# A fused attention, gated layer and 8-expert layer: new order tables, expert operands inside the order, last first-layer column in expert PSUM banks

## The chip, the cores and the metric

The kernel runs on one core of a Trainium2 chip. The metric is the device time of one execution in microseconds (us), the median over several runs. PE is TensorE (matmuls), DVE is VectorE, ACT is ScalarE, POOL is GpSimd, SP issues the DMAs.

## What is computed

Three stages, one behind the other, on 1152 tokens of width 512:

```python
def _moe_ref(x, w_gate, w_val, w_out):
    gate = 1.0 / (1.0 + np.exp(-(x @ w_gate)))
    val = x @ w_val
    return (gate * val @ w_out).astype(np.float32)

def _moe2_ref(x, w_gate, w1, w2):          # N=1152, D=512, E=8, F=1024
    logits = x @ w_gate
    P = np.exp(logits - logits.max())
    for _ in range(8):
        P /= P.sum(1, keepdims=True) + 1e-09
        P /= P.sum(0, keepdims=True) + 1e-09
        P *= N / E
    out = np.zeros((N, D), dtype=np.float32)
    for e in range(E):
        h = np.maximum(x @ w1[e], 0.0)
        out += P[:, e:e + 1] * (h @ w2[e])
    return out.astype(np.float32)

def reference(q, k, v, moe, moe2):
    x = _attn_ref(q, k, v)                 # softmax attention, queries pooled by 2
    x = _moe_ref(x, *moe)                  # the first layer
    return _moe2_ref(x, *moe2)             # the expert stage
```

## The kernel before

**Number format.** Every fp32 operand of a matmul is held as a pair: a high part (an ACT copy that rounds to the matmul's format) and a low part (source minus high part, a DVE or POOL subtraction). Such a pair is called a split here. A product then takes three matmuls: high x high, high x low, low x high (`three`, L835 to L837; in the second product L1281, L1285, L1286).

**Stages.** Attention comes first and is not touched. The first layer follows: gate and value products, then a loop over four column blocks of w_out (`for c in range(KD)`, L898). Each block accumulates 108 matmuls of 384 columns in a PSUM tile `pso` of three banks, and `take_x` (L888) copies blocks 0 to 2 to SBUF tiles `xs`. The last block (c = 3) ends at 514.97 us.

**Seam.** Between the first layer and the expert stage the expert operands are made from the four `xs` columns: sums and differences of halves of x for Winograd's form of Strassen's scheme, each split (`combine_x0`, `combine_x1`, L932 to L962, with `split_x`, L113, L114; three more, `rest_of_x`, later). `combine_x1` reads block 3 out of its PSUM tile (DVE, L951 and L955). Only then is the pool `pso` closed and the expert pool `ps_f` opened, whose eight banks X0, X1, Y0, Y1, B0, B1, y0, y1 are a tile each (psX, psY, psB, psy). `ready_banks` (L1380, the step "set") writes B0 and B1 once to set them up.

**Expert stage.** 16 half-experts hx = 0 to 15 (an expert's halves), each 46.2 us long: two first products (mi = 0, 1; seven products of 2 x 12 matmuls of 288 columns) and one second product, which consists of seven products k = 0, 2, ..., 7 of 2 x 12 matmuls of 256 columns (halves n = 0 and 1 of a product go to the two banks of a key, such as X0 and X1) and the "plain" block of 12 matmuls of 512 columns into y0 behind product 0. Product 0 goes to key a, product 2 to c, 3 to a, 4 to B, 5 to a, 6 to c, 7 to a; a is X in even half-experts and Y in odd ones. After product 0, ACT copies its two banks to B0 and B1 (`go`); product 4 adds to them there. DVE takes each result out of PSUM, weighted by the routing, into `acc` (`take`, L1239; "tk 3 1 0" is the take of product 3's half n = 1, "tk p" that of the plain block).
Beside this run the works for what comes next: weights are loaded by SP (`raw_w`), summed by POOL (`sm`), copied by ACT and subtracted by DVE (`w_one`, `w_two`, L1018, L1021); the hidden halves likewise (`hb`, `hp`). The routing (logits, then eight turns of row and column normalisation: `ra` on DVE, `cc`, a matmul with ones into y1, `rb` on DVE) is woven into half-experts 0 and 1.

**What sets the order.** The program's order on each engine is fixed. Each piece is a `step` with a due time `when`, a table entry of nanoseconds added to it (SHIFT), the time it holds its engine (`takes`), the time to its result (`lasts`) and the buffers it gets and frees. `arrange` (L180 to L227) simulates all engines by these numbers and always starts the step that can begin first; equal times go by `when`. DVE and POOL steps with `port=True` share one port there: while one holds it no other begins. The core of the choice:

```python
                    t = max(free[eng], s["at"], port if s["port"] else 0.0)
...
                        key = t, s["when"], s["seq"]
...
            if s["port"]:
                port = t + s["takes"]
```

## Time and profile before

| | us |
|---|---|
| runs of the kernel | 1288.32, 1292.27, 1292.31 (median 1292.27) |
| the profiled execution, own time | 1287.63 |
| its span | 1285.4 |
| TensorE busy in the span | 1244.3 (97%) |
| last column of the first layer ends | 514.97 |
| first matmul of the expert stage | 522.41 |

The profile is of one execution. A wait is an engine's idle time, put down to the instruction that ended it. The granted clock is that of TensorE: 1.00 is its upper level, 2.4 GHz, and a stretch at half of it is the lower, 1.2 GHz; a mean between stands for a mixture. Matmuls overlap, so what a matmul costs is the distance from its start to the next one's start, not its duration. Times in the timeline are from the span's start.

### The profile page before, as it was taken

What the parts mean: (1) busy time and instruction counts of PE and PEld (TensorE: products, weight loads), DVE (VectorE), ACT (ScalarE), POOL (GpSimd) and SP (SyncE); (2) the same over time, 40 slices, a digit from 0 to 9 for tenths busy, and PEclk for the clock granted to TensorE, in tenths of its full rate; (3) what the DMA queues carried; (4) which work ended last, traced back from release to release, by engine and by line L of the source; (5) the groups of instructions that cost most, each with busy time, mean ns of one, the idle gap of its engine ahead of it and who ended that gap; (6) DMA issues with size and microseconds to landing.
All of it is one profiled execution on the core that took longest, in us unless ns stands there. A gap on an engine that the chain in (4) does not pass through costs nothing.

```text
span 1285.4 us, 23682 instructions
## 1 busy us (share of the span) xinstructions
PE 1244.3 (97%) x8924; PEld 1210.1 (94%) x8924; DVE 1074.5 (84%) x1955; ACT 779.6 (61%) x1772; POOL 737.6 (57%) x751
## 2 busy tenths in 40 slices
PE   8999999989999999699999999999999999999998
PEld 6889999989999999699999999999999999999998
DVE  7999999997666662799988898898898898889887
ACT  8999999974333331655466457547546646745753
POOL 7788888664343423462673565565466467456552
PEclk9999999999999999799999999999999999999999
DMA  5112220013222321111111101211111120121102
GB/s 160 44 47 56 57 57 20 27 34 106 91 83 83 98 82 50 33 34 50 43 41 50 66 30 38 66 34 50 50 34 50 50 66 18 50 67 33 45 23 75
DMA packets 61202, 70.48 MB, mean 55 GB/s; under 512 B 3360, under 2 KB 47776, under 8 KB 61088
## 3 DMA queue, kind: packets, MB, share of 16 engines
q1 hardware_dynamic: 61088, 68.97, 17.4%
q8 instruction: 70, 1.15, 0.4%
q14 instruction: 44, 0.36, 0.1%
HBM read 66.60 MB, written 2.36 MB: 54 GB/s over the span
## 4 chain that ended last, share of the span: by engine, by line
PE 65%; DVE 26%; ACT 6%; issue 2%; DMA 1%; POOL 0%; SPq 0%; DVEq 0%; ACTq 0%; POOLq 0%
DVE hb L1021 9%; DVE acc L1239 4%; PE psb L837 4%; PE psb L836 4%; PE psb L835 4%; PE psY L835 4%; PE psY L837 4%; PE psY L836 4%; PE psX L835 4%; PE psX L837 4%; PE psX L836 4%; DVE pT L455 3%; PE psg L474 3%; PE psg L435 2%; PE psY L1281 2%; PE psX L1281 2%
## 5 line engine op out<-in xcount | busy, mean ns | idle before, releaser
L1021 POOL TENSOR_TENSOR sm<-raw_w 128x256 f32<-128x256 f32 x128 | 120.0, 952 | 81.9 <-DMA raw_w<-in_moe_w_dram 52.7
L1021 DVE TENSOR_TENSOR hb<-sm,hb 128x512 fp32r<-128x512 f32 x128 | 128.0, 1010 | 39.5 <-ACT hb L1018 39.5
L1018 ACT ACTIVATE w_two<-raw_w 128x512 fp32r<-128x512 f32 x96 | 60.7, 634 | 151.5 <-DMA raw_w<-in_moe_w_dram 113.5
L474 PE MATMUL psg<-pT,vs 128*128 128x256 f32 (+1 forms) x576 | 133.1, 318 | 0.2
L1021 POOL TENSOR_TENSOR sm<-xs 128x512 f32<-128x512 f32 x40 | 60.4, 1509 | 94.5 <-ACT xs L1018 94.5
L1281 PE MATMUL psY<-w_two,hb 128*128 128x256 f32 x384 | 109.2, 284 | 5.0 <-DVE acc L1239 4.1
L1281 PE MATMUL psX<-w_two,hb 128*128 128x256 f32 x384 | 109.0, 284 | 5.1 <-DVE acc L1239 5.1
L1018 ACT ACTIVATE w_two<-sm 128x512 fp32r<-128x512 f32 x128 | 80.8, 631 | 51.1 <-POOL sm L1021 34.3
L455 DVE TENSOR_TENSOR pT<-psg,pT 128x384 fp32r<-128x384 f32 x192 | 101.8, 550 | 7.8 <-ACT pT L451 5.9
L1286 PE MATMUL psX<-w_two,hb 128*128 128x256 f32 x384 | 108.3, 282 | 0.0
L1286 PE MATMUL psY<-w_two,hb 128*128 128x256 f32 x384 | 108.2, 282 | 0.0
L1285 PE MATMUL psY<-w_two,hb 128*128 128x256 f32 x384 | 108.2, 282 | 0.0
L1285 PE MATMUL psX<-w_two,hb 128*128 128x256 f32 x384 | 108.1, 282 | 0.0
L435 PE MATMUL psg<-ident,p 128*128 128x128 f32 x648 | 104.3, 273 | 0.8 <-DVE pT L455 0.3
L837 PE MATMUL psb<-x,w_gv 128*128 128x384 f32 x288 | 96.3, 334 | 3.7 <-POOL w_gv L150 3.7
L1021 DVE TENSOR_TENSOR w_two<-sm,w_two 128x512 fp32r<-128x512 f32 x128 | 94.7, 749 | 2.4 <-ACT w_two L1018 0.6
L1018 ACT ACTIVATE hb<-sm 128x512 fp32r<-128x512 f32 x128 | 78.5, 626 | 29.9 <-POOL sm L1021 27.8
L835 PE MATMUL psb<-x,w_gv 128*128 128x384 f32 x288 | 96.3, 334 | 0.0
L836 PE MATMUL psb<-x,w_gv 128*128 128x384 f32 x288 | 96.2, 334 | 0.0
L474 PEld LDWEIGHTS psg<-pT,vs 128*128 128x128 f32 x576 | 91.1, 189 | 3.7 <-DVE pT L455 0.7
L451 ACT ACTIVATE pT<-psg 128x384 fp32r<-128x384 f32 x192 | 90.6, 499 | 5.9 <-PE psg L435 4.6
L1021 POOL TENSOR_TENSOR sm<-raw_w,sm 128x256 f32<-128x256 f32 x96 | 84.2, 884 | 3.7
(279 smaller groups left out, 4786.6 us busy)
## 6 DMA issues: line engine op xcount, KB each, us to landing
raw_w<-in_moe_w_dram SPq DMA_DIRECT2D x64, 512.0 KB, 3.6
raw_gv<-in_moe_w_gate_dram SPq DMA_DIRECT2D x12, 512.0 KB, 3.6
raw_gv<-in_moe_w_val_dram SPq DMA_DIRECT2D x12, 512.0 KB, 3.5
raw_o<-in_moe_w_out_dram SPq DMA_DIRECT2D x12, 512.0 KB, 3.4
vr<-in_v_dram SPq DMA_DIRECT2D x16, 288.0 KB, 2.8
kr<-in_k_dram SPq DMA_DIRECT2D x15, 288.0 KB, 2.8
qr<-in_q_dram SPq DMA_DIRECT2D x15, 256.0 KB, 3.9
out_dram<-acc SPq DMA_DIRECT2D x8, 256.0 KB, 2.2
```

What stands on the lines that cost most here:

```text
L435: nc.tensor.transpose(have["tpp", i, u, g][:, n * P:(n + 1) * P], have["p", i, u][:, jj * P:(jj + 1) * P], ident)
L451: nc.scalar.activation(out=p_parts(i, u, g)[0], in_=turned(i, u, g), func=AF.Copy)
L455: nc.vector.tensor_tensor(out=lo, in0=turned(i, u, g), in1=f(hi), op=ALU.subtract)
L474: nc.tensor.matmul(have["pv", i, j, n][:, 0:HALF[n][1]], have["vs", i, j][:, jj].rearrange("p a d -> p (a d)"), have["pT", i, j, n][s][:, ...
L835: nc.tensor.matmul(ps, wh, xh, start=first, stop=False, skip_group_check=more)
L836: nc.tensor.matmul(ps, wh, xl, start=False, stop=False, skip_group_check=more)
L837: return nc.tensor.matmul(ps, wl, xh, start=False, stop=last, skip_group_check=more).ins
L1018: nc.scalar.activation(out=out_, in_=in_, func=func)
L1021: eng.tensor_tensor(out=out_, in0=a, in1=b, op=op)
L1281: nc.tensor.matmul(out_, h[:, 0, cols], w[:, 0], start=(begins and kk + m == 0), stop=False, skip_group_check=True,)
L1285: nc.tensor.matmul(out_, h[:, 0, cols], w[:, 1], start=False, stop=False, skip_group_check=True)
L1286: nc.tensor.matmul(out_, h[:, 1, cols], w[:, 0], start=False, stop=(m == 1), skip_group_check=True)
```

## The change

Three parts. First, `arrange` serves the port by arrival: among port steps that could start at the same time, the one that asked first goes first (`asks`), and a step holds the port for a time of its own (`port=570` and the like) rather than for as long as it holds its engine. The durations are set anew, half-experts 0 and 1 have table entries of their own, the whole SHIFT table has new numbers (about 360 of them), and the eight routing turns and the first weight buffers get other places. Second, the expert operands are made by steps in the same order (`inputs`), with the letters a to i for the operands of x's first (0) and second (1) half of columns and h, l for high and low part; x3 is the last column's way out of PSUM, now on ACT. Third, the last column block accumulates in a tile `psz` of three banks of the expert pool, which the expert stage then uses as Y1, y0 and y1.

```diff
@@ SHIFT, one line of it before and after
-    "tk 6 0 0": 9739, "tk 6 1 0": 6392, "tk 6 1 1": -443, "tk p": 251, "wh 0 1 0": -9339, "wh 0 1 1": -2683,
...
+    "tk p": 27398, "wh 0 1 0": -2595, "wh 0 1 1": -3229, "wh 0 1 2": -3554, "wh 0 1 3": 567, "wh 0 2 0": 7154,
@@ arrange
-                    t = max(free[eng], s["at"], port if s["port"] else 0.0)
+                    asks = max(free[eng], s["at"])
+                    t = max(asks, port) if s["port"] else asks
...
-                        key = t, s["when"], s["seq"]
+                        key = t, asks if s["port"] else t, s["when"], s["seq"]
...
-                port = t + s["takes"]
+                port = t + s["port"]
...
-                    own = s["takes"]
+                    own = s["lasts"] + 80 if s["port"] and s["name"] not in u["after"] else s["takes"]
@@ the loop over column blocks
-            ps = ps_b.tile([P, 3, 512], F32, tag="b", name="pso")
...
+            if c < KD - 1:
+                ps = ps_b.tile([P, 3, 512], F32, tag="b", name="pso")
+            else:
+                pbs.close()
+                ps_f = ctx.enter_context(tc.tile_pool(name="ps_f", bufs=1, space=PSUM, reuse_waits="tile"))
+                bank = {k: ps_f.tile([P, 512], F32, tag=k, name=f"ps{k[0]}") for k in ("B0", "B1", "X0")}
+                ps = ps_f.tile([P, 3, 512], F32, tag="z", name="psz")
+                bank.update((k, ps[:, n]) for n, k in enumerate(("Y1", "y0", "y1")))
+                bank.update((k, ps_f.tile([P, 512], F32, tag=k, name=f"ps{k[0]}")) for k in ("X1", "Y0"))
@@ step
+        own = key if isinstance(name, str) else f"{name[1]}|{key}"
...
-            steps, name, eng, when * 1e3 + SHIFT.get(key, 0), takes, lasts, emit, deps, list(gets), [*dict.fromkeys(uses)], list(after),
+            steps, name, eng, when * 1e3 + SHIFT.get(own, SHIFT.get(key, 0)), takes, lasts, emit, deps, list(gets), [*dict.fromkeys(uses)], list(after),
@@ weights, total, split: new durations and holds, such as
-                ("sum", *name, x), "POOL", when((1, 2, 4, 5)[x]) - 1.5, 1270, 1270, lambda x=x: total(x), deps, [("cv", cv[x])],
-                [cv[x], *uses], port=True,
+                ("sum", *name, x), "POOL", when((1, 2, 4, 5)[x]) - 1.5, 1250, 1290, lambda x=x: total(x), deps, [("cv", cv[x])],
+                [cv[x], *uses], port=1150,
@@ combine_x0, combine_x1 and rest_of_x fall away; in their place
+    def inputs():
...
+        t = START
+        split("a0", x12[:, 0], low, 0, t - 12, least=t - 12)
+        less("d0", t - 14, lambda: high(0), lambda: low(1), lambda: high(0), (), 0, 1)
+        less("e0", t - 9, lambda: low(0), lambda: low(1), lambda: low(0), ["a0h", "a0l"], 0, 1)
+        split("c0", xb[0][:, 0], high, 1, t - 13)
+        split("b0", xc[0][:, 0], high, 0, t - 10, ["d0"], least=t - 10.6)
+        split("g0", xc[0][:, 1], low, 0, t - 8, ["e0"], least=t - 10.6)
+        split("h0", xb[0][:, 1], low, 1, t - 7)
+        less("f0", t - 10, lambda: high(1), lambda: high(1), lambda: high(0), ["d0", "c0h", "c0l"], 0, 1, eng="POOL")
+        split("i0", xd[:, 0], high, 1, t - 6, ["f0"], eng="POOL", least=t - 7.5)
+        for n, w in ((0, TB), (1, HT - TB)):
+            step(
+                f"d1{n}", "DVE", t - 2, (470, 270)[n], (560, 360)[n],
...
+                ), (), (), [("x", 2)], least=t, ps=("Y1", "y0")[n],
+            )
+        step("x3", "ACT", t - 2, 1050, 1140, take_x3, (), (), [("x", 3)], least=t, ps="Y1 y0 y1")
+        split("b1", xc[1][:, 0], high, 2, t - 1, ["d10", "d11"])
+        split("c1", xb[1][:, 0], high, 3, t, ["x3"])
...
+        less("f1", t + 2.5, lambda: high(3), lambda: high(3), lambda: high(2), ["c1h", "c1l", "d10", "d11"], 2, 3, eng="POOL")
+        split("i1", xd[:, 1], high, 3, t + 4, ["f1"], eng="POOL")
+        split("a1", x12[:, 1], low, 2, t + 5, eng="POOL")
@@ the start and the turns of the routing
-    START, PERIOD, PHASE = 14.0, 45.4, 11.25
+    START, PERIOD, PHASE = 20.0, 45.4, 11.25
...
-    TURNS = [(0, 2, k) for k in (2, 4, 6, 8)] + [(1, 0, k) for k in (2, 5)] + [(1, 1, k) for k in (1, 4)]
-    step("set", "PE", START - 1, 460, 700, ready_banks, ps="B0= B1=", least=START - 1)
+    TURNS = [(0, 2, 4), (0, 2, 7), (1, 0, 2), (1, 0, 5), (1, 1, 1), (1, 1, 4), (1, 2, 2), (1, 2, 4)]
+    step("set", "PE", START - 1, 460, 700, ready_banks, ps="B0= B1=", least=START)
...
-    begin = {("w2", k): 4000.0 + 1000 * k for k in range(3, 9)}
+    begin = {("w2", k): t * 1e3 for k, t in enumerate((2, 2, 4, 4, 5.5, 20.3, 20.3, 20.3, 20.3))}
+    begin.update({("w1", k): 2e3 for k in range(2)})
...
-        for s in arrange(steps, stock, 30e3, begin, {("x", 0): ("m", 0), ("x", 1): ("m", 1)}):
+        for s in arrange(steps, stock, 30e3, begin, {("x", k): ("m", k) for k in range(4)}):
```

PE's matmuls come in the same order as before, but for the `cc` of the routing. What moved on the other engines, at three places (the number behind a tile's name tells the tiles apart; it differs between the two programs, so psY_5686 before and psz_5486 after hold the same half of product 0).

ACT in the second product of half-expert 5, before. The two `go` copies are the rows psB<-psY:

```order
L1018 ACTIVATE psB_5687<-psY_5685 128x512
L1018 ACTIVATE hb_5667<-sm_5649 128x512
L1018 ACTIVATE hb_5673<-xs_5431 128x512
L1018 ACTIVATE hb_5672<-xs_5431 128x512
L1018 ACTIVATE hb_5676<-sm_5650 128x512
L1018 ACTIVATE hb_5668<-sm_5654 128x512
L1018 ACTIVATE psB_5688<-psY_5686 128x512
L1018 ACTIVATE w_one_5655<-raw_w_5647 128x256
```

And of the change:

```order
L1055 ACTIVATE psB_5484<-psz_5486 128x512
L1055 ACTIVATE hb_5646<-sm_5627 128x512
L1055 ACTIVATE hb_5648<-sm_5624 128x512
L1055 ACTIVATE hb_5643<-sm_5626 128x512
L1055 ACTIVATE w_one_5631<-raw_w_5623 128x256
L1055 ACTIVATE w_one_5630<-raw_w_5621 128x256
L1055 ACTIVATE psB_5483<-psY_5488 128x512
```

Before, the copy of Y0 stood first and that of Y1 behind five splits' copies; now the copy of Y1, out of psz, is first and that of Y0 behind three copies of `hb` and two of `w_one`.

DVE in the same second product, from the last splits of `hb` before product 2's takes on, before. The row acc<-psy is "tk p":

```order
L1021 TENSOR_TENSOR hb_5673<-xs_5431,hb_5673 128x512
L1239 SCALAR_TENSOR_TENSOR acc_5691<-psy_5689,pr_69,acc_5691 128x512
L1239 SCALAR_TENSOR_TENSOR acc_5691<-psX_5683,pr_69,acc_5691 128x256 x2
L1239 SCALAR_TENSOR_TENSOR acc_5691<-psX_5684,pr_69,acc_5691 128x256 x2
L1239 SCALAR_TENSOR_TENSOR acc_5691<-psY_5685,pr_69,acc_5691 128x256 x2
L1021 TENSOR_TENSOR hb_5671<-sm_5649,hb_5671 128x512
L1021 TENSOR_TENSOR w_two_5660<-sm_5653,w_two_5660 128x512
L1021 TENSOR_TENSOR hb_5669<-sm_5650,hb_5669 128x512
L1239 SCALAR_TENSOR_TENSOR acc_5691<-psB_5687,pr_69,acc_5691 128x256
L1239 SCALAR_TENSOR_TENSOR acc_5691<-psY_5686,pr_69,acc_5691 128x256 x2
```

And of the change, where the row acc<-psz of 128x512 is "tk p":

```order
L1276 SCALAR_TENSOR_TENSOR acc_5659<-psX_5487,pr_69,acc_5659 128x256 x2
L1058 TENSOR_TENSOR w_one_5631<-raw_w_5623,w_one_5631 128x256
L1276 SCALAR_TENSOR_TENSOR acc_5659<-psY_5488,pr_69,acc_5659 128x256 x2
L1058 TENSOR_TENSOR hb_5652<-sm_5626,hb_5652 128x512
L1276 SCALAR_TENSOR_TENSOR acc_5659<-psz_5486,pr_69,acc_5659 128x256
L1058 TENSOR_TENSOR hb_5641<-sm_5624,hb_5641 128x512
L1276 SCALAR_TENSOR_TENSOR acc_5659<-psz_5486,pr_69,acc_5659 128x256
L1058 TENSOR_TENSOR w_two_5633<-sm_5625,w_two_5633 128x512
L1058 TENSOR_TENSOR w_two_5639<-raw_w_5623,w_two_5639 128x512
L1276 SCALAR_TENSOR_TENSOR acc_5659<-psB_5483,pr_69,acc_5659 128x256
L1276 SCALAR_TENSOR_TENSOR acc_5659<-psB_5484,pr_69,acc_5659 128x256 x2
L1276 SCALAR_TENSOR_TENSOR acc_5659<-psz_5486,pr_69,acc_5659 128x512
```

Before, "tk p" stood ahead of all other takes, and the second half of product 3 (psY_5686) behind three splits in a row; now the takes of product 3 stand between the splits one by one, and "tk p" comes last, behind two `hb` and two `w_two` splits.

ACT at the seam, before, from the first operand made of column 0 on (xs_5630 is the last column's copy, made by DVE):

```order
L113 ACTIVATE xc0_5608<-xs_5124 128x576
L113 ACTIVATE xb0_4973<-xs_5280 128x576
L113 ACTIVATE xc0_5608<-xs_5124 128x576
L113 ACTIVATE xb0_4973<-xs_5280 128x576
L1018 ACTIVATE w_two_5660<-sm_5649 128x512
L113 ACTIVATE xd_5610<-xs_5280 128x576
L113 ACTIVATE xc1_5609<-xs_5431 128x576
L113 ACTIVATE xb1_4974<-xs_5630 128x576
L113 ACTIVATE xc1_5609<-t3_5637 128x576
L1018 ACTIVATE w_two_5661<-raw_w_5646 128x512
L1018 ACTIVATE xb1_4974<-xs_5630 128x576
```

And of the change (xs_5658 is the last column, now copied by ACT):

```order
L1055 ACTIVATE xc0_5618<-xs_5124 128x576 x2
L1055 ACTIVATE xd_5620<-xs_5280 128x576
L1055 ACTIVATE w_two_5633<-sm_5625 128x512
L1055 ACTIVATE w_two_5638<-raw_w_5621 128x512
L1055 ACTIVATE w_two_5639<-sm_5624 128x512
L1055 ACTIVATE w_two_5640<-raw_w_5622 128x512
L1055 ACTIVATE xs_5658<-psz_5486 128x1152
L1055 ACTIVATE xc1_5619<-xs_5431 128x576
L1055 ACTIVATE xb1_4974<-xs_5658 128x576
L1055 ACTIVATE psB_5483<-psX_5485 128x288
```

Before, the copies of xc0, xb0 and xd stood behind the last column's end; now xc0 (both), xd and the first four `w_two` stand ahead of the copy of the last column, which is followed by xc1 and xb1 and the first `go` of the expert stage.

## Rows read from the trace of the kernel before

**Rows 1.** The profile page's first part: busy us, share of the span, instructions by engine.
```profile
PE 1244.3 (97%) x8924; PEld 1210.1 (94%) x8924; DVE 1074.5 (84%) x1955; ACT 779.6 (61%) x1772; POOL 737.6 (57%) x751
```

**Rows 2.** Waits of TensorE from 505 us on: us in total, times, longest.
```profile
PE psB L1380 <- DVE xs L955: 7.4, 1, 7.4
PE psX L1281 <- DVE acc L1239: 5.1, 7, 1.0
PE psy L1472 <- DVE cs L1425: 4.2, 2, 2.3
PE psY L1281 <- DVE acc L1239: 4.1, 6, 0.7
...
PE psY L1281 <- DVE acc L1237: 0.9, 1, 0.9
```

**Rows 3.** Stretches of 25 us: length, busy time and count by engine, clock, DMA share.
```profile
515.00:540.00 25.00, 15.22 (x80) 14.59 (x81) 19.87 (x25) 14.37 (x29) 10.90 (x8) 0.73 0.07 21
...
565.00:590.00 25.00, 22.75 (x174) 22.54 (x173) 24.11 (x73) 6.65 (x15) 12.51 (x15) 0.93 0.13 39
```

**Rows 4.** Timeline of TensorE at the seam: start, us, engine, line, operation.
```profile
522.41 1.19 PE L1380 MATMUL psB<-xa 128*128 128x512 f32 x2 [7.44 <-DVE xs L955]
523.40 0.44 PE L835 MATMUL psX<-xa,w_two 128*128 128x288 f32 x1
...
527.24 0.43 PE L836 MATMUL psY<-xa,w_two 128*128 128x288 f32 x1
...
527.64 0.30 PE L835 MATMUL psY<-xa,w_two 128*128 128x288 f32 x1
...
528.31 0.29 PE L837 MATMUL psY<-xa,w_two 128*128 128x288 f32 x1
530.59 0.40 PE L835 MATMUL psX<-xc,w_two 128*128 128x288 f32 x1 [1.99 <-ACT psB L1018]
```

**Rows 5.** Timeline of VectorE at the seam.
```profile
520.92 1.34 DVE L955 COPY xs<-pso 128x1152 f32<-128x1152 f32 x1
```

**Rows 6.** Timeline of VectorE, then TensorE, in the second product of half-expert 2.
```profile
664.33 1.78 DVE L1021 TENSOR_TENSOR hb<-xs,hb 128x512 fp32r<-128x512 f32 x1
666.03 0.74 DVE L1239 SCALAR_TENSOR_TENSOR acc<-psy,pr,acc 128x512 f32<-128x512 f32 x1
...
669.04 1.10 DVE L1021 TENSOR_TENSOR hb<-sm,hb 128x512 fp32r<-128x512 f32 x1
670.07 1.22 DVE L1021 TENSOR_TENSOR w_two<-sm,w_two 128x512 fp32r<-128x512 f32 x1
671.21 1.22 DVE L1021 TENSOR_TENSOR hb<-sm,hb 128x512 fp32r<-128x512 f32 x1
...
672.75 0.86 DVE L1239 SCALAR_TENSOR_TENSOR acc<-psX,pr,acc 128x256 f32<-128x256 f32 x2
...
671.40 0.28 PE L1281 MATMUL psX<-w_two,hb 128*128 128x256 f32 x1
...
672.71 0.28 PE L1286 MATMUL psX<-w_two,hb 128*128 128x256 f32 x1
673.67 0.39 PE L1281 MATMUL psX<-w_two,hb 128*128 128x256 f32 x1 [0.68 <-DVE acc L1239]
```

**Rows 7.** Groups by line and form, VectorE, 660 to 1260 us: count, busy, mean ns.
```profile
L1021 DVE TENSOR_TENSOR hb<-sm,hb 128x512 fp32r<-128x512 f32 x104 | 105.2, 1021 | 35.5 <-ACT hb L1018 35.5
L1021 DVE TENSOR_TENSOR w_two<-sm,w_two 128x512 fp32r<-128x512 f32 x104 | 76.9, 749 | 1.7
```

**Rows 8.** Timeline of ScalarE in the same second product.
```profile
661.81 0.59 ACT L1018 ACTIVATE psB<-psX 128x512 f32<-128x512 f32 x1
662.33 0.40 ACT L1018 ACTIVATE w_one<-raw_w 128x256 fp32r<-128x256 f32 x1
663.89 0.63 ACT L1018 ACTIVATE w_two<-sm 128x512 fp32r<-128x512 f32 x1 [1.16 <-POOL sm L1021]
664.42 0.62 ACT L1018 ACTIVATE w_two<-raw_w 128x512 fp32r<-128x512 f32 x1
```

More of the change, by code (lines that the diff above doesn't have):

```diff
@@ L226, in arrange, with entry @@
         return [s for _, _, s in sorted(out, key=lambda x: x[:2])]
-    def entry(steps, name, eng, when, takes, lasts, emit, deps, gets, frees, after, port=False, least=0.0):
+    def entry(steps, name, eng, when, takes, lasts, emit, deps, gets, frees, after, port=0, least=0.0):
         steps[name] = dict(
@@ L985, in moe_stack_kernel, with step @@
         "hp": [hp_p.tile([P, 2, 2, HT - HW], F32R, tag="hp", name="hp") for _ in range(4)],
-        "m": [spare[0], xs[2], xs[1], spare[1]],
+        "m": [*xs, misc.tile([P, N], F32, tag="m", name="xs")],
     }
-    bank = {f"{k}{n}": ps_f.tile([P, 512], F32, tag=f"{k}{n}", name=f"ps{k}") for k in "XYBy" for n in range(2)}
     acc = o_p.tile([P, NT, DM], F32, tag="acc", name="acc")
+    stock["w2"] = [stock["w2"][k] for k in (0, 1, 6, 7, 8, 2, 3, 4, 5)]
     have, steps, chain, last_pe, owner = {}, {}, {}, [], {}
-    def step(name, eng, when, takes, lasts, emit, deps=(), gets=(), uses=(), after=(), port=False, least=0.0, ps=""):
+    def step(name, eng, when, takes, lasts, emit, deps=(), gets=(), uses=(), after=(), port=0, least=0.0, ps=""):
         deps = list(deps)
@@ L1103, in split @@
             lambda: join(nc.vector, have[tile_][:, 1], src(), f(have[tile_][:, 0]), ALU.subtract),
-            [("hh", *name, o)], (), [tile_, *uses], port=True,
+            [("hh", *name, o)], (), [tile_, *uses], port=570,
         )
@@ L1349, in second_product @@
         takes(7, A22, a, 4, 0, True, True)
-    def rest_of_x():
-        x22, x21 = (spare[0][:, n * HT:(n + 1) * HT] for n in range(2))
-        x11, x12_ = xs[2][:, HT:N], xs[2][:, 0:HT]
-        return (
-            (xb[1][:, 1], x22, nc.vector), (x12[:, 1], x12_, nc.gpsimd), (xd[:, 1], x21, nc.gpsimd),
-        ), lambda: nc.gpsimd.tensor_tensor(out=x21, in0=x21, in1=x11, op=ALU.subtract)
-    parts, difference = rest_of_x()
-    step(
-        "x21", "POOL", START + 1, 1400, 1430, difference, (), (), [("x", 0), ("x", 1)],
-        port=True, least=START,
-    )
@@ L1377, in ready_banks @@
+    inputs()
     def ready_banks():
```

107 lines of the change are left out of this document (44 added, 63 removed), and 121 rows, old and new, of the table SHIFT.

## Prediction

> **What bounds the kernel now.** First the table of engines: TensorE is busy 1244.3 us, 97% of the span [rows 1]; no other engine is over 84%. So time can only come out of TensorE's gaps, or out of stretches where it runs slowly. Second the table of waits for TensorE, from the start of the expert stage on [rows 2]. It has three kinds of entries: one of 7.4 us, where `ready_banks` (L1380) waits for DVE's copy of the last first-layer column; two that come to 4.2 us, where the `cc` matmul of the routing waits for DVE; and 13 short ones, together 9.2 us, where product 5 of a second product (L1281) waits for DVE's `take` (L1239). Third the stretches of 25 us [rows 3]: from 515 to 540 TensorE is busy for only 15.22 us, at a granted clock of 0.73; from 565 to 590 for 22.75 us at 0.93. A busy engine at half clock is lost time that no wait shows. So the three places that bear on this change are the seam at 515 us, the routing in half-experts 0 and 1, and the 13 recurring waits.
>
> **The seam.** The last column ends at 514.97 (522.41 less the gap of 7.44 [rows 4]). DVE copies it out only at 520.92, for 1.34 us [rows 5], and `ready_banks` needs its banks free, so it starts at 522.41 [rows 4]. The matmuls behind it step by 0.24 us (523.40 to 527.24 is 16 steps), then by 0.134 (527.64 to 528.31 is 5), and at 530.59 there is a second gap, of 1.99 us, with the step at 0.24 behind it [rows 4]. What the seam costs: in the 25 us stand 80 matmuls [rows 3], two of `ready_banks` at about 0.25 (half of the 0.5 that each takes here at the lower clock [rows 4]) and 78 at 0.134, 10.9 us of work. 25 - 10.9 = 14.1 us are lost.
> After the change the last column lies in banks Y1, y0 and y1 of the expert pool. `ready_banks` writes B0 and B1, which no earlier work holds, so TensorE runs on at 515.0. The first product uses X, the second Y; Y1 has to be drained first, by d10, d11 (DVE) and x3 (ACT), which is 0.47, 0.3 and about 1.2 us by rows of like width. They end near 517.1, and the second product's Y1 half is due at 517.7. The operands that do not need the last column (a0 to i0) and the first weights are made while it runs. I walked the rest of the first product by the same durations: each operand is there before its product, by 0.2 to 2 us. So I take the whole **-14.1**. Cover: if the chain d10, d11, b1, c1, g1, h1 falls behind by over 2 us, the clock falls as it did behind the gap at 530.59, and that is rival C. The lower end is half, -7; the upper end is -14.1, since no more was lost.
>
> **The routing.** Before: 4.2 us of waits for `cs`, 0.9 for a take in half-expert 1 [rows 2], some 0.3 for slow first matmuls, and behind the first gap the clock at 0.93 for 25 us [rows 3], which by the same step of 0.24 for 0.134 over 13 matmuls is 1.4: together **-6.8**. The change spreads the eight turns to (0,2,4) ... (1,2,4), so each `ra`/`rb` has more time. What comes new: banks Y1, y0 and y1 are one tile, psz, and a tile is waited for as a whole. So `cc`, which writes y1, now also waits until DVE has taken Y1 or y0. The nearest row for one such wait is the take of 512 columns, 0.74 us [rows 6]. I find three among the logits and their transposes, 0.6 to 0.8 each: **+2.2**; and five in the two half-experts, 0.3 to 1.2: **+4.0**. Bounds: nothing for each (if DVE was through already), or 1.2 for all eight, 9.6.
>
> **The recurring wait.** In half-expert 2 the first half of product 5 is issued from 671.40 to 672.71, so the next could come at 672.83; it comes at 673.67 and its first matmul takes 0.1 longer [rows 6]: 0.94. The take at 672.75 released it; ahead of that on DVE stand three splits of 1.10, 1.22 and 1.22 us, beside GpSimd's sums. 13 x 0.95 = **-12.4**, if the new order removes it. In the built order those splits now stand elsewhere, and in even half-experts (first key X) I find no wait left. Bounds: 0 and -12.4.
>
> **What the one tile costs in odd half-experts.** There the first key is Y, so Y1 is in psz, beside the plain block's y0. Let 0 be the moment when TensorE ends the plain block's issue.
> First wait: the `go` copy of Y1 (ACT, the order's first excerpt) waits for the whole tile, so for the plain block's last matmul, about 0.2. Behind it ACT does, start to start, the copy 0.52, three splits' copies at 0.53, two of 256 columns at 0.31, then `go` of Y0, 0.59 [rows 8]: 0.2 + 0.52 + 1.59 + 0.62 + 0.59 = 3.5. Product 3 wants bank Y0 at 2 x 1.44 = 2.88. Wait 0.65, slow first matmul 0.1: **0.75**.
> Second wait: product 5's second half writes Y1, so the whole tile, and must wait for `tk p`, the take of y0. Before, that stood early (666.03, some 3 us after the plain block [rows 6]); now it is behind four splits (second excerpt). TensorE is ready at 2.88 + 0.75 + 5 x 1.44 = 10.8. DVE gets product 3's first half at 5.25 and then has two takes (0.39 each, from the pair of 0.86 [rows 6]), a split, a take, a split, a take, two splits, three takes and `tk p`, 0.74. With 0.94 for a split of `hb` and 0.67 for one of `w_two` (the means less the 0.08 by which they overlap [rows 7]): 5.25 + 7 x 0.39 + 2 x 0.94 + 2 x 0.67 + 0.74 = 11.95. Wait 1.2, slow matmul 0.1: **1.3**.
> Together 2.05 in each of half-experts 3, 5, ..., 13, for the last has no weights to make: 6 x 2.05 = **+12.3**. Bounds: all four splits at 0.67, 1.5 each, +9; all four at the 1.14 start to start of the splits at 670.07 and 671.21 [rows 6], 3.4 each, +20. The means hold both kinds, so I stay with them.
>
> **Sum.** 1287.6 - 14.1 - 6.8 - 12.4 + 2.2 + 4.0 + 12.3 = 1272.8, and 2 more for tile waits at places that I did not walk (63 in all cross banks): 1274.8. That is against the profiled execution, which lies 4.7 us under the median of the runs; they spread over 4 us, so I add half of it: **1277**.
>
> **A rule against the change.** By the trace a DVE split beside a short GpSimd sum costs 1.10 to 1.22 against means of 0.75 to 1.02, and one, at 664.33, cost 1.78 [rows 6, 7]. The Trainium skill, SBUF — State Buffer, section "SBUF: two separate sides", states more: DVE with two SBUF inputs and GpSimd share a port pair as an exclusive lock, and the loser blocks for the other's whole instruction. By that rule each of the four splits that meets a long sum would cost what the one at 664.33 did, which is rival D's way; the mean of 1.02 says that most do not meet one.
>
> **The rivals.**
> A, as above, 1271 to 1284: chance 0.53.
> B, the tile waits cost little, because DVE's queue is ahead of TensorE and `tk p` comes in time. For it: DVE is idle before many takes. Against: 11.95 is 1.2 late by means, not by the worst rows. Without the 12.3: 1265, and 1261 if part of the 6.2 goes as well. Chance 0.15.
> C, the seam gives only half: ACT has five copies of 0.6 to 1.2 us between 515 and 520, GpSimd the long differences f1 and i1, and one of them over 2 us late halves the clock again. 1277 + 7 = 1284. Chance 0.15.
> E, the change does not do what its port rule says: the recurring wait stays in the seven even half-experts, 7 x 0.95 = 6.7, beside the odd ones. Together with C that is 1277 + 6.7 + 7 = 1291, no change. Chance 0.08.
> D, the other side: in odd half-experts all four splits meet sums, at 1.14 each, so `tk p` is 2.6 us late (3.4 less 0.75); TensorE then comes back at half clock, which behind the gap of 1.99 was 0.24 for 0.134 over some 13 matmuls, 1.4 [rows 4]; where behind gaps of 0.68 it did not happen [rows 6]. 0.75 + 2.6 + 1.4, and a later catch-up of 0.8 in the next product, 5.5 for each, 33 for 12.3: 1277 + 20.7 = 1298. It decides from about 5.2 us an odd half-expert on. For it: DVE is 84% busy [rows 1] and the takes come behind splits. Against: three contended splits in a row are in the rows, four are not. Chance 0.09.
>
> **How the numbers follow.** What a measurement can tell here is about 0.3%, 3.9 us. A, B and C are faster by more: 0.83. E is the same: 0.08. D is slower: 0.09. The range reaches from B's lower end, 1260, over A, C and the bound of +20 for the tile (1285) to 1290, just under E; D and most of E are left out.
>
> **What would show it.** Right: `ready_banks` starts within 1 us of the last column's end and the stretch 515 to 540 shows TensorE busy over 24 us at a clock near 1.00; no L1281 wait in even half-experts; in odd ones two waits, one for ACT's psB of about 0.65 and one for the take of y0 of about 1.2, repeating every 92 us; routing waits below 4 us. Wrong: waits of over 2 us in odd half-experts with a lowered clock (D), none there (B), gaps between 516 and 530 (C), or L1281 still waiting in even ones (E).

## The result and the profile after

The changed kernel takes 1273.84 us (median of 4 runs, 1273.15 to 1274.44) against 1291.96 us before (median of the 4 runs taken beside it): a ratio of 0.9866, 95% interval 0.9847 to 0.9885. So it is faster by 18 us, 1.3%. The profiled execution took 1273.15 us, the one before 1287.63.

For the rest of this text one number per kernel is needed that leaves the first two stages out. Executions differ by up to 4 us before the seam is reached, in stages that no kernel here touches: the last matmul of the last column starts at 514.63 us in the kernel before, at 515.67 in the changed one, and anywhere from 515.4 to 518.8 in the experiments. **Stage time** below is the time from the start of that matmul to the start of the program's last matmul, in the profiled execution: 766.2 us before (514.63 to 1280.86), 750.6 after (515.67 to 1266.25). The difference is 15.6 us.

Where it went, by four milestones on TensorE:

| from ... to | before | after | difference | forecast |
|---|---|---|---|---|
| last column to first logits matmul | 26.2 | 12.6 | -13.6 | -14.1 |
| to the last plain matmul of half-expert 0 | 21.8 | 24.0 | +2.1 | +2.2 |
| to that of half-expert 2 | 99.9 | 97.4 | -2.5 | -6.8 + 4.0 |
| to the end | 618.3 | 616.6 | -1.7 | -12.4 + 12.3 |

TensorE's waits from 505 us on in the changed kernel (us in total, times, longest), to be held against [rows 2]:

```profile
PE psz L1318 <- DVE acc L1276: 4.9, 6, 0.8
PE psY L1318 <- ACT psB L1055: 2.8, 6, 0.5
PE psz L1540 <- DVE acc L1274: 1.6, 1, 1.6
PE psz L1455 <- ACT xs L1055: 1.0, 2, 0.5
PE psz L1540 <- ACT xs L1055: 0.6, 1, 0.6
PE psz L903 <- ACT xs L1055: 0.6, 1, 0.6
PE psX L903 <- DVE xs L1058: 0.5, 1, 0.5
PE psX L903 <- ACT psB L1055: 0.4, 1, 0.4
PE psX L1318 <- DVE acc L1274: 0.2, 1, 0.2
```

The 7.4 us of `ready_banks` and the 13 waits for a take are gone. In their place stand two groups of six, both naming the new tile or its neighbours. The same two stretches as in [rows 3]:

```profile
515.00:540.00 25.00, 23.01 (x167) 20.41 (x166) 22.13 (x31) 17.47 (x42) 14.08 (x12) 1.00 0.20 57
...
565.00:590.00 25.00, 24.44 (x187) 23.84 (x186) 21.84 (x61) 15.77 (x37) 9.87 (x10) 1.00 0.15 43
```

167 matmuls instead of 80 in the first, and the clock at its upper level throughout. The seam itself on TensorE, for [rows 4]:

```profile
515.67 0.33 PE L905 MATMUL psz<-gt,w_o 128*128 128x384 f32 x1
515.85 0.63 PE L1448 MATMUL psB<-xa 128*128 128x512 f32 x2
516.31 0.30 PE L903 MATMUL psX<-xa,w_two 128*128 128x288 f32 x1
...
520.07 0.40 PE L903 MATMUL psX<-xc,w_two 128*128 128x288 f32 x1 [0.41 <-ACT psB L1055]
```

`ready_banks` follows the last column without a gap, and of the gap of 1.99 us before product 2 only 0.41 is left.

An odd half-expert (3), whose plain block is issued up to 695.08: ACT, then DVE, then TensorE.

```profile
695.29 0.58 ACT L1055 ACTIVATE psB<-psz 128x512 f32<-128x512 f32 x1 [3.54 <-PE psz L1355]
695.78 1.66 ACT L1055 ACTIVATE hb<-sm 128x512 fp32r<-128x512 f32 x3
697.35 0.71 ACT L1055 ACTIVATE w_one<-raw_w 128x256 fp32r<-128x256 f32 x2
697.96 0.58 ACT L1055 ACTIVATE psB<-psY 128x512 f32<-128x512 f32 x1
...
699.82 1.19 DVE L1058 TENSOR_TENSOR w_one<-raw_w,w_one 128x256 fp32r<-128x256 f32 x1
...
704.90 1.26 DVE L1276 SCALAR_TENSOR_TENSOR acc<-psB,pr,acc 128x256 f32<-128x256 f32 x3
706.08 0.74 DVE L1276 SCALAR_TENSOR_TENSOR acc<-psz,pr,acc 128x512 f32<-128x512 f32 x1
...
698.59 0.39 PE L1318 MATMUL psY<-w_two,hb 128*128 128x256 f32 x1 [0.47 <-ACT psB L1055]
...
706.87 0.39 PE L1318 MATMUL psz<-w_two,hb 128*128 128x256 f32 x1 [0.82 <-DVE acc L1276]
```

ACT stands idle for 3.54 us until the plain block is done, then works off what is queued, and product 3 waits for the copy of Y0: 0.47 of idle time, a start that comes 0.63 late, and 0.1 more because the first matmul behind the wait takes longer, 0.73 in all. Product 5's second half waits for `tk p` at 706.08: 0.82 idle, 0.98 late, 1.08 in all. This repeats every 92.3 us, 47.06 from the plain block of an odd half-expert to the next and 45.25 from that of an even one.

### The profile page after: what moved, and what is told of

Read it like the earlier page. It is cut to its first block, busy times and chain, and to the rows that moved or that the text cites. A ratio compares the mean times of both kernels' runs of the same rounds, so it can differ in the third digit from the quotient of the medians.

```text
span 1271.4 us, 23695 instructions
## 1 busy us (share of the span) xinstructions
PE 1241.3 (98%) x8924; PEld 1206.2 (95%) x8924; DVE 1071.4 (84%) x1954; ACT 780.0 (61%) x1773; POOL 710.8 (56%) x751
## 4 chain that ended last, share of the span: by engine, by line
PE 75%; DVE 15%; ACT 5%; issue 3%; POOL 1%; DMA 1%; SPq 0%; DVEq 0%; ACTq 0%; POOLq 0%
PE psb L905 4%; PE psb L904 4%; PE psb L903 4%; PE psX L903 4%; PE psX L905 4%; PE psX L904 4%; PE psX L1318 3%; PE psX L1323 3%; PE psX L1322 3%; PE psg L542 3%; DVE pT L523 3%; PE psg L503 3%; DVE acc L1276 3%; PE psz L903 2%; PE psz L904 2%
## 5 line engine op out<-in xcount | busy, mean ns | idle before, releaser
L1058 POOL TENSOR_TENSOR sm<-xs 128x512 f32<-128x512 f32 x64 | 92.3, 1452 | 182.2 <-ACT xs L1055 155.4
L1055 ACT ACTIVATE w_two<-sm 128x512 fp32r<-128x512 f32 x128 | 77.8, 629 | 156.5 <-POOL sm L1058 134.8
L1058 POOL TENSOR_TENSOR sm<-raw_w 128x256 f32<-128x256 f32 x128 | 102.9, 824 | 125.5 <-DMA raw_w<-in_moe_w_dram 74.5
L1058 DVE TENSOR_TENSOR hb<-sm,hb 128x512 fp32r<-128x512 f32 x128 | 116.7, 934 | 24.9 <-ACT hb L1055 24.8
L1058 DVE TENSOR_TENSOR w_two<-sm,w_two 128x512 fp32r<-128x512 f32 x128 | 112.8, 890 | 5.0 <-ACT w_two L1055 5.0
L1058 POOL TENSOR_TENSOR sm<-raw_w,sm 128x256 f32<-128x256 f32 x96 | 90.5, 956 | 0.3
L1058 DVE TENSOR_TENSOR w_two<-raw_w,w_two 128x512 fp32r<-128x512 f32 x96 | 75.2, 785 | 17.0 <-ACT w_two L1055 15.3
L1058 DVE TENSOR_TENSOR hb<-xs,hb 128x512 fp32r<-128x512 f32 x96 | 87.5, 924 | 0.0
L503 PEld LDWEIGHTS psg<-ident,p 128*128 128x128 f32 x648 | 78.6, 140 | 6.2 <-issue 1.2
L495 POOL TENSOR_SCALAR p<-p,sum 128x672 f32<-128x672 f32 x72 | 59.6, 828 | 38.5 <-ACT sum L491 34.8
```

The source lines that it names most:

```text
L503: nc.tensor.transpose(have["tpp", i, u, g][:, n * P:(n + 1) * P], have["p", i, u][:, jj * P:(jj + 1) * P], ident)
L1055: nc.scalar.activation(out=out_, in_=in_, func=func)
L1058: eng.tensor_tensor(out=out_, in0=a, in1=b, op=op)
```

## Experiments

Each experiment changes one thing of the changed kernel unless it says otherwise. Where the text says that an engine's order stays, no row of it moves.

**e1: three tiles for the three banks.**

```diff
-                ps = ps_f.tile([P, 3, 512], F32, tag="z", name="psz")
-                bank.update((k, ps[:, n]) for n, k in enumerate(("Y1", "y0", "y1")))
+                bank.update((k, ps_f.tile([P, 512], F32, tag=k, name=f"ps{k[0]}")) for k in ("Y1", "y0", "y1"))
+                ps = [bank[k] for k in ("Y1", "y0", "y1")]
...
-            copy(xt[3].rearrange("p (n w) -> p n w", n=3), ps[:, :, 0:TB])
+            for n in range(3):
+                copy(xt[3][:, n * TB:(n + 1) * TB], ps[n][:, 0:TB])
```

> The changed kernel with its order row for row, but banks Y1, y0 and y1 are three tiles instead of the one psz; the last column's way out (x3) is three ACT copies of 384 columns instead of one of 1152. Theory (the odd half-experts pay 0.63 + 0.98 us each for waits on a bank that nobody uses): both waits in half-experts 3 to 13 go, 6 x 1.6 = 9.7 us; the cc waits of 0.7 and 1.75 us and the wait of 0.7 at 535 go too; the two logits waits of 0.7 may stay, since they write banks that ACT still reads. 1273.8 - 9.7 - 3.2 = 1261, range 1259 to 1264. Rival (the waits come from DVE and ACT being late, the tile only names them): the waits stay with the real bank, 1271 to 1274.

Measured: 1259.88 us, 0.9754 of the kernel before (0.9735 to 0.9773); stage time 736.8, 13.7 less than the changed kernel. Its waits from 505 us on, all of them:

```profile
PE psy L1541 <- DVE cs L1494: 1.1, 1, 1.1
PE psX L903 <- DVE xs L1058: 0.5, 1, 0.5
PE psX L1318 <- DVE acc L1274: 0.2, 1, 0.2
```

Both waits of the odd half-experts are gone, every half-expert from 3 on takes 45.25 us, and the logits waits went too. So the tile cost 47.06 - 45.25 = 1.81 us in each odd one, 0.2 more than the 0.63 + 0.98 of the expectation, which left out the 0.1 of the slow first matmul behind each wait. The wait of 1.6 us of a `cc` did not go: the same `cc` still waits 1.1, now put down to DVE's row sums `cs`. The tile is the cause: the order and the work are the same but for `x3` (three copies for one), only what the program guards as one piece differs. This is the best version of the study, 32 us under the kernel before.

The Trainium skill, PSUM — Partial Sum Buffer, section "PSUM bank collisions raise a hardware error", asks for PSUM to be guarded by bank and quadrant, by bank as the simple version. The one tile guarded three banks together, more than that rule asks; 13.7 us is what this cost here.

**e2: the last column in the first layer's pool again** (part 3 undone, banks a tile each; `ready_banks` now opens the expert pool, behind `d10`, `d11` and `x3`).

```diff
-            if c < KD - 1:
-                ps = ps_b.tile([P, 3, 512], F32, tag="b", name="pso")
-            else:
...
+            ps = ps_b.tile([P, 3, 512], F32, tag="b", name="pso")
```

> The changed kernel with its order row for row, but the last column accumulates in the first layer's pool again, which is given up behind d10, d11 and x3; eight banks are a tile each, as in the kernel before. So part 3 alone is undone. Theory (most of the seam comes from what is made ahead of it, part 3 only hides the copy of the last column): ready_banks starts some 1.5 to 2 us behind the last column instead of 0.3, with little or no slow clock behind it; against e1 +1.5 to +3.5 us, so 1262 to 1265. Rival (part 3 is what closes the seam): the gap of 7 us and the half clock come back, +9 to +12 against e1, 1270 to 1273.

Measured: 1265.75 us (0.9802, 0.9785 to 0.9819), stage time 740.4: 3.6 us over e1 in the profiled executions, 5.9 by the medians. The waits' first row, the stretch and the DVE row that releases TensorE:

```profile
PE psB L1444 <- DVE xs L1050: 2.5, 1, 2.5
```

```profile
515.00:540.00 25.00, 22.54 (x151) 20.87 (x150) 20.63 (x27) 18.10 (x40) 12.04 (x9) 0.93 0.13 43
```

```profile
520.72 0.36 DVE L1050 TENSOR_TENSOR xs<-pso,xs 128x192 f32<-128x192 f32 x1 [1.20 <-ACT xs L1047]
```

The gap is 2.5 us, not 7.4, but the clock falls behind it (0.93), which the expectation had not counted, so the result lies just over its range. The rival is out: up to the first logits matmul the place of the last column is worth 3.7 us (16.0 against e1's 12.3) of the seam's 13.6.

**e3 and e4: one table entry each.** In e3 the plain block's take comes earlier on DVE, in e4 the copy of Y0 earlier on ACT.

```diff
-    "tk p": 27398,
+    "tk p": 18000,
```
```diff
-    "go 0": 26582,
+    "go 0": -6000,
```

> The changed kernel with one table entry changed: the take of the plain block (tk p) is due 9.4 us earlier in half-experts 2 to 15. On DVE it moves from behind product 4's takes to behind product 2's; nothing else moves in the odd half-experts 3 to 13. Theory (product 5 waits for this take through the common tile): the wait of 0.98 us at product 5 goes in six half-experts, -5.9 us, the one of 0.63 at product 3 stays; 1268, range 1267 to 1270. Rival (DVE is late there in any case, by its splits beside GpSimd's sums): the wait stays but names another take, 1272 to 1275.

> The changed kernel with one table entry changed: in half-experts 2 to 15 the copy of bank Y0 (or X0) to B0 is due earlier, so on ACT it stands ahead of the copy of Y1 and of five splits' copies instead of behind them. Theory (product 3 waits for this copy because ACT stands at the whole tile): the wait of 0.63 us at product 3 goes in six half-experts, -3.8 us, the one of 0.98 stays; 1270, range 1269 to 1272. Rival (the copy of Y1, which must wait for the plain block, now delays product 3's second half or a split of hb): the wait only moves, 1273 to 1275.

Measured: 1274.46 us and 1275.92 us, stage times 752.1 and 750.5. Both expectations missed: no gain from either; the rivals' times were nearer. Three rows of e3's waits:

```profile
PE psz L1318 <- DVE acc L1276: 2.9, 7, 0.9
...
PE psX L1322 <- DVE w_two L1058: 1.6, 1, 1.6
PE psz L903 <- DVE acc L1276: 1.1, 1, 1.1
```

and one of e4's:

```profile
PE psz L1318 <- DVE acc L1276: 7.3, 6, 1.2
```

In e3 the wait at product 5 is gone, but the take now stands ahead of product 3's second half, which writes Y1 and so waits for it: 0.98 became 0.48, six times over. The 3 us went into three new waits, which come once each: for a late split of `w_two` in half-expert 2 (1.8 us), for a take at the first product behind half-expert 7 (1.4), and for this same take in the last half-expert (1.2), 4.4 together. In e4 the first wait is gone and the second grew from 0.98 to 1.38 (with 0.25 more for a late split): the pair of half-experts takes 92.3 us as before. The two waits lie on one chain, set by when DVE takes y0.

**e5: both, with the take as the first behind the plain block** (`"tk p": 251`, `"go 0": -6000`).

> The changed kernel with two table entries changed, for half-experts 2 to 15: the plain block's take is due 27 us earlier, so on DVE it is the first take behind the plain block, and the copy of Y0 (X0) stands ahead of that of Y1 on ACT, as in e4. Theory after e3 and e4 (both waits of an odd half-expert come from the one tile, but they lie on one chain: the take of y0 ends when DVE's queue lets it, so the second wait grows by what the first gives back; only where DVE takes y0 at once, about 1 us behind the plain block and 4 us before Y1 is written again, does the half-expert run without a wait): the pair of half-experts falls from 92.3 to some 90.6 us, -1.6 us six times over, -9.7; from the last column to the end 750.6 - 9.7 = 741. Rival (DVE's queue is the limit in odd half-experts whatever the tile): the wait stays at one of the products, 748 to 751.

Measured: 1275.79 us, stage time 751.4; missed; the time is next to the rival's 748 to 751, but the wait is not where the rival had it. An even half-expert (4), TensorE and DVE:

```profile
744.67 0.39 PE L1318 MATMUL psz<-w_two,hb 128*128 128x256 f32 x1 [0.73 <-DVE acc L1276]
```

```profile
743.88 0.74 DVE L1276 SCALAR_TENSOR_TENSOR acc<-psz,pr,acc 128x512 f32<-128x512 f32 x1
```

Over e1's 45.25 us the odd half-experts keep only 0.7 of their 1.8, but in even ones Y1 is product 2's bank, written 1.44 us behind the plain block, and now that write waits for the take: 1.0 each. While the tile is one, the take is in somebody's way at each of the three places tried; e1 ends that.

**e6: the kernel before, with only the late takes moved ahead.**

```diff
-    "tk 4 1 0": 1909, "tk 4 1 1": 1586,
+    "tk 4 1 0": -4000, "tk 4 1 1": -3900,
```

> The kernel BEFORE with two table entries changed (tk 4 1 0 and tk 4 1 1): the takes of product 3's second half are due about 6 us earlier, so on DVE they stand ahead of two or three of the splits that they stood behind; ACT, POOL and TensorE keep their order. Theory (the 13 recurring waits of 0.95 us are a matter of DVE's order at this one place, not of how much DVE has to do): they go, -12.4 us, 1279.6, range 1278 to 1282. Rival (a split of hb that moves back is then late, so TensorE waits for it instead): 1286 to 1293.

Measured: 1314.02 us, slower than the kernel before (1.0172, 1.0154 to 1.0189) and beyond what either side expected. Its two largest waits, and the DVE row behind the one of half-expert 2 that ends at 683.34:

```profile
PE psX L1285 <- DVE w_two L1021: 17.4, 8, 2.2
PE psY L1285 <- DVE w_two L1021: 16.2, 8, 2.6
```

```profile
682.61 0.68 DVE L1021 TENSOR_TENSOR w_two<-sm,w_two 128x512 fp32r<-128x512 f32 x1
```

The 13 waits for a take are gone, and TensorE waits 2.4 us for the split of `w_two` that product 5 needs. The planner arranges all rows anew, so two entries moved more than the two takes: four takes of product 4 now stand ahead of that split as well, which product 5 does not need and which hold DVE for 4 x 0.39 = 1.6 us. So moving the takes in this way only exchanges the wait for a longer one. Without those four the split would have been some 0.8 us late (an estimate, 2.4 less 1.6); such an order was not tried.

**e7: operands late.**

```diff
-                name + "h", "ACT", when, 585, 680, lambda: copy(out_[:, 0], src(i)), deps, (), [("x", i)], least=least,
+                name + "h", "ACT", when, 585, 680, lambda: copy(out_[:, 0], src(i)), deps, (), [("x", i)], least=max(least, START),
```

and `least=START` for the differences (`less`).

> The changed kernel, but no expert operand is made before the last column has ended (every operand step has the last column's end as its earliest time; the first weights are still made during the column). Theory (the seam closes because the operands are made ahead, the banks alone don't do it): ACT and DVE have some ten more pieces of 0.6 to 0.75 us behind the last column, product 2 and those after it wait 3 to 5 us in all and the clock falls for a while, as at 530.59 in the kernel before: from the last column to the end 750.6 + 5 to 8, so 755 to 759. Rival (the free banks B0, B1, X0 close the seam, operands come in time either way): 750 to 752.

Measured: 1285.23 us (0.9942, 0.9925 to 0.9959), stage time 761.6: 11.0 us given back, over the expected range. Its largest wait, and the stretch:

```profile
PE psX L904 <- DVE xc L1058: 5.1, 1, 5.1
```

```profile
515.00:540.00 25.00, 17.77 (x108) 16.98 (x107) 20.82 (x25) 14.10 (x28) 10.00 (x6) 0.86 0.05 18
```

The free banks were there, and the seam opened all the same: operands made ahead are worth more than the banks. Up to the logits it is 9.1 us, and the clock is low again behind the 5.1.

**e8: the planner's old key.**

```diff
-                        key = t, asks if s["port"] else t, s["when"], s["seq"]
+                        key = t, s["when"], s["seq"]
```

> The changed kernel with the old key in the planner: equal start times at the port go by due time alone, not by who asked first; tables, durations and hold times stay new. On DVE and POOL some sixty rows move, most of them at the seam and in half-expert 0; in half-experts 3 to 13 the takes and splits of the second product stand as before. Theory (the new tables and hold times carry the gain, the rule by itself hardly anything): from the last column to the end 750 to 754. Rival (the rule is what takes the recurring wait out): 0.95 us comes back in the even half-experts, 757 or more.

Measured: 1298.84 us, slower than the kernel before (1.0056, 1.0042 to 1.0071); stage time 771.6, 21 over the changed kernel. Two rows of its waits:

```profile
PE psz L1540 <- DVE cs L1493: 7.1, 2, 6.5
PE psY L1318 <- ACT psB L1055: 6.3, 7, 3.5
```

Both sides missed. The recurring wait does not come back in even half-experts, so the rule alone is not what took it out. But the order that comes from the new tables under the old key puts the row sums of a routing turn behind the splits of half-expert 1, and `cc` waits 6.5 us. The table fits its rule: what either is worth alone can't be read from this.

**e9 to e12: POOL made busy beside the splits.** The base is e1. In the changed kernel POOL is idle (for weights on their way) while DVE makes the four splits between the takes of products 3 and 4, and these cost 0.68 each; before, they cost 1.10 to 1.22 beside POOL's sums [rows 6]. In half-expert 3, the last of the four on DVE and POOL's next sum:

```profile
704.29 0.68 DVE L1058 TENSOR_TENSOR w_two<-raw_w,w_two 128x512 fp32r<-128x512 f32 x1
...
705.29 3.49 POOL L1058 TENSOR_TENSOR sm<-raw_w 128x256 f32<-128x256 f32 x5 [3.69 <-DMA raw_w<-in_moe_w_dram]
```

These four experiments fill that time with work on a scratch tile.

```diff
             join(nc.gpsimd, *t[x]())
+            if kind == 2 and m % 2 == 1 and x == 3 and 2 <= name[0] <= 14:
+                for _ in range(6):
+                    nc.gpsimd.tensor_tensor(out=extra, in0=ident, in1=ones, op=ALU.add)
```

(e10: 14 times `nc.gpsimd.memset(extra, 1.0)`; e11: four additions of 256 columns of `xa`, e12: three of 512, both from half-expert 3 on.)

> e1 with six extra POOL additions of two 128x128 constants into a scratch tile, behind the last weight sum of half-experts 2 to 14: 2.4 to 2.8 us of POOL work by the 0.46 us that such an addition took elsewhere, in the time in which POOL otherwise waits for the next weights, and in which DVE makes the four splits between the takes of products 3 and 4. Orders of all other engines stay. Theory (the recurring wait of the kernel before is gone because the new order leaves POOL idle beside these splits, so that they cost 0.60 us start to start instead of 1.1): the splits go to about 1.0 to 1.1; in even half-experts the last take of product 3 comes some 1.5 to 2 us later than in e1 where TensorE has 1.3 us in hand, so a wait of 0.3 to 0.8 us comes back in seven half-experts; in odd ones there is more in hand and nothing happens. From the last column to the end 736.8 + 2 to 6: 739 to 743. Rival (the interleaved order of takes and splits is enough by itself): 736.5 to 738.

> The control to e9: in the same place fourteen POOL memsets of the same scratch tile (0.2 us each elsewhere, so some 2.4 us), which write to SBUF but read nothing from it. Theory (POOL slows a DVE split by reading SBUF beside it): the splits stay near 0.60 us start to start and the time from the last column to the end stays at 736.5 to 738. Rival (any POOL instruction that touches SBUF slows them, writes too): as e9, 739 to 743.

> e1 with four extra POOL additions of 256 columns (the shape of a weight sum, 0.74 us alone) behind the last weight sum of half-experts 3 to 14; half-expert 2 is left out, since there e9 and e10 lost 4 us by making POOL late for the next half-expert. Theory from e9 (a POOL addition and a DVE split shut each other out for a whole instruction, whichever began first; an addition of 128 columns fits beside one take, so there it was POOL that waited): an addition of 256 columns is longer than the take beside it and runs into the next split's start, so the splits between the takes go from 0.68 to about 0.95. TensorE does not pay for that, because in e1 the last take of product 3 in an even half-expert ends 2.6 us before product 5 wants its bank: from the last column to the end 736.5 to 738.5. Rival (the splits stay at 0.68 as in e9, POOL always waits): additions of over 1.2 us, same time. Rival for the time: each 0.3 us on DVE reaches TensorE, 14 us.

> As e11, with three additions of 512 columns (1.3 us alone, the shape of a sum of hidden halves). Theory: the first two splits between the takes go to 1.2 to 1.6 us, the last take of product 3 comes some 1.5 to 2 us later, still inside the 2.6 us; what comes behind (the next weights' sums on POOL, 1 us later than in e1) may cost up to 0.5 us a half-expert: from the last column to the end 737 to 743. Rival (a wait as in the kernel before, 0.5 to 1 us at product 5 in every even half-expert): the wait names DVE's take at L1281's place, 741 to 744.

| | us | stage time | splits between the takes | mean of an extra |
|---|---|---|---|---|
| e1 | 1259.88 | 736.8 | 0.68 | |
| e9, 6 x 128 columns | 1269.92 | 745.3 | 0.68, the fourth mostly 0.95 | 0.758 |
| e10, 14 memsets | 1265.38 | 740.9 | 0.68 | 0.206 |
| e11, 4 x 256 columns | 1261.17 | 739.2 | 0.75 to 1.22 | 0.986 |
| e12, 3 x 512 columns | 1273.08 | 750.3 | 1.29 to 1.38, the fourth 1.21 | 1.511 |

In e9 and e10 over 4 us were lost between the plain blocks of half-experts 2 and 3 alone, since the extras of half-expert 2 made POOL's next sums late; behind that e10 lost nothing and e9 0.2 to 0.6 us a half-expert. So e10's time lies in its rival's range, but not for the rival's reason: the splits stayed at 0.68. e9's expectation missed: there three of the four splits did not suffer, POOL did. Its extras, and e10's, by group (count, busy, mean ns):

```profile
L1100 POOL TENSOR_TENSOR extra<-ident,ones 128x128 f32<-128x128 f32 x78 | 59.1, 758 | 5.1
```

```profile
L1100 POOL MEMSET extra<- 128x128 f32 x182 | 37.4, 206 | 9.7
```

An addition of this size took 0.46 alone and 0.76 here in the mean; a memset, which reads nothing, took its 0.2 as ever. In e12 it is mutual. POOL and DVE in half-expert 4, and its largest waits:

```profile
743.81 4.69 POOL L1100 TENSOR_TENSOR extra<-xa 128x512 f32<-128x512 f32 x3
```

```profile
744.33 1.32 DVE L1059 TENSOR_TENSOR hb<-sm,hb 128x512 fp32r<-128x512 f32 x1
745.58 0.47 DVE L1280 SCALAR_TENSOR_TENSOR acc<-psX,pr,acc 128x256 f32<-128x256 f32 x1
745.97 1.38 DVE L1059 TENSOR_TENSOR hb<-sm,hb 128x512 fp32r<-128x512 f32 x1
```

```profile
PE psY L1326 <- DVE w_two L1059: 5.2, 6, 0.9
PE psX L1326 <- DVE w_two L1059: 5.1, 6, 0.9
```

Three additions of 1.3 us fill 4.69 instead of 3.9, two splits of 0.68 take 1.32 and 1.38, and the take between them, which reads PSUM, takes its 0.47. TensorE then waits about 1.1 us in each of twelve half-experts, 13.5 us in all, for the `w_two` split that e6 had made late. Both sides missed the time (744 at most, measured 750), and the rival named the wrong wait: it is the split, not the take. e11 shows the middle, three of its four splits in half-expert 6 and its largest wait:

```profile
833.45 0.75 DVE L1059 TENSOR_TENSOR hb<-sm,hb 128x512 fp32r<-128x512 f32 x1
...
835.67 0.83 DVE L1059 TENSOR_TENSOR w_two<-sm,w_two 128x512 fp32r<-128x512 f32 x1
836.42 1.22 DVE L1059 TENSOR_TENSOR w_two<-raw_w,w_two 128x512 fp32r<-128x512 f32 x1
```

```profile
PE psX L903 <- ACT psB L1056: 1.3, 2, 1.1
```

The four take 3.6 us together, as long as the three of the kernel before (3.5), and no wait at product 5 comes back; TensorE pays 2.3 us in all, a little over the 738.5 expected.

So the wait for the take came back in none of the four. What they show is the other half: once the takes stand between the splits, the split of `w_two` is the next to be late, and POOL's reads beside it decide whether it is (1.1 us in e12, nothing in e11). e6, with the takes ahead and POOL's sums left where they were, waited for that same split. That the new order both puts the takes between the splits and keeps POOL's sums away from them is read from the trace; what either does alone was not separated, and which table entries do it was not tried.

## Why the prediction was right

The forecast was 1277 us, range 1260 to 1290; measured 1273.84. Rival A, the likeliest, is what happened, by its total and by the waits that it named; two of its terms were wrong, and in part they cancelled.

e1, which is the changed kernel without the common tile, lets the sum be taken apart by the milestones. What a term gained without the tile is e1 less the kernel before; what the tile cost is the changed kernel less e1.

| term | stretch | forecast | measured |
|---|---|---|---|
| seam | last column to the plain block of half-expert 0 | -14.1 | 34.3 - 48.0 = -13.7 |
| routing | to that of half-expert 2 | -6.8 | 96.8 - 99.9 = -3.1 |
| recurring wait | to the end | -12.4 | 605.7 - 618.3 = -12.6 |
| tile, up to there | as the seam | +2.2 | 36.5 - 34.3 = +2.2 |
| tile, five routing places | as the routing | +4.0 | 97.4 - 96.8 = +0.6 |
| tile, odd half-experts | as the recurring wait | +12.3 | 616.6 - 605.7 = +11.0 |
| places not walked | | +2 | |
| sum | | -12.8 | -15.6 |

**The seam**, the largest term, was right, and for the reason given. The trace has the signs that were named: `ready_banks` right behind the column, and the clock at 1.00 from 515 to 540. It was put down to the operands and weights made ahead together with the free banks; e7 and e2 show that both are needed and which is larger (9.1 and 3.7 up to the logits).

**The routing** is where the forecast was lucky. Its two terms came to -2.8 and the stretch measured -2.5, but neither term was right: without the tile the routing gained 3.1 us and not 6.8, since waits stayed that the sum had taken as gone (in e1 1.1 us for `cs` and 0.5 for `xs`), and the tile cost 0.6 there and not 4.0. Of the five places one cost 1.75 in the changed kernel, but that is the `cc` that waits 1.1 in e1 too.

**The recurring wait**, -12.4: gone in even half-experts, and in e1 in odd ones too, for the 12.6. The prediction put the wait down to the three contended splits ahead of the take and said that they stand elsewhere in the new order, which the trace shows. But e11, with these splits together as long as before and no wait, says that their contention alone does not bring it back once the takes stand between them. How much the order did, and how much POOL's absence, stays open.

**The tile**, +12.3 as 6 x (0.75 + 1.3): measured 6 x (0.73 + 1.08) = 10.9. Each wait was found at its place and with its releaser, and the first at its size. In the second two errors met: a split in this place was taken at 0.94 and 0.67 from start to start, and with POOL idle all four took 0.60, below the lower bound, 0.8 less in all; and a `w_one` split that met POOL's sums (1.19 us at 699.82) held product 3's first take until 5.85 behind the plain block, not 5.25, 0.6 more. The two waits were also added as if they were independent, which e4 refutes: without the first the second grows, and the pair takes as long.

**The 2 us for places not walked** were not there. The tile was put too dear by 6.7 us and the routing's gain too high by 3.7: that the total is out by only 2.8 us is in part the one error against the other. Against the profiled execution 1 us of it was hidden, because the last column came that much later in this execution.

**The rivals.** B (the tile costs little) was out by the tile's 10.9 us, and e1, which has no such waits because it has no such tile, took 1259.9, a little under B's 1261 to 1265. C did not happen: one wait of 0.41 between 516 and 530. D needs 5.2 us an odd half-expert; it was 1.8, and POOL was idle beside the four splits. E is out: no wait in even half-experts.

**The rule against the change.** By the Trainium skill, SBUF — State Buffer, section "SBUF: two separate sides", a DVE instruction with two SBUF inputs and a GpSimd instruction that reads SBUF lock each other out for a whole instruction. The traces agree: in e12 splits and additions both lengthen (0.68 to 1.38, 1.3 to 1.5 in the mean), and in e10, where POOL reads nothing, neither does. It did not lead to rival D, since the new order keeps POOL's reads away from these splits.

## What to carry to other kernels

A tile is what waits are counted by: if independent banks are put into one tile for the sake of one copy, every later use of one bank waits for the others, and none of the four orders tried here hid that (13.7 us; three copies cost nothing visible). When one stage hands over to the next, look first at what can be made before the last result is there, and then at whether its space is free; both had to be done, and a gap at TensorE can cost more than its length, by the clock behind it (2.5 us of gap and 3.7 of time in e2). Two waits that name different releasers may lie on one chain: take one away before adding them. And a sum that comes out can hide two wrong terms: the run with the tile taken out is what told them apart here.

## What was not expected of the hardware

A DVE split with both inputs in SBUF and a POOL addition lengthened each other, and which of them lost changed with the addition's size: additions of 128 columns left three of four splits at 0.68 and grew from 0.46 to 0.76 themselves (e9); additions of 512 columns made splits of 0.68 take 1.29 to 1.38 (e12); memsets took 0.206 and left the splits at 0.68 (e10). That the short additions fit into the time of a take, 0.47, and so lose, is a reading of these rows and was not tested. Takes, which read one operand from PSUM, stayed at 0.47 beside all of them.

Behind e2's gap of 2.5 us at TensorE the granted clock fell to its lower level for a while (0.93 over the 25 us), behind e7's of 5.1 us too (0.86); behind the gaps of 0.4 to 1.6 us in the changed kernel it stayed at 1.00. The length of the gap does not decide alone: e6 has a gap of 2.2 us in each of the half-experts 2 to 14 and one of 2.6 in half-expert 1, and behind all of these the clock stayed at 1.00:

```profile
715.00:740.00 25.00, 22.78 (x179) 22.02 (x178) 22.71 (x38) 8.33 (x15) 19.32 (x20) 1.00 0.12 43
```

What sets these gaps apart from e2's the runs do not show.
